# Sixteen decode buffers in the memory of a ring that starts later, both gates from tanh, and signs made off VectorE, in a top-32 attention and two gated feed-forward layers

## The chip, the cores and the metric

The kernel runs on one core of a Trainium2 chip. Its engines are TensorE (PE, matmuls; its weight loads are shown as PEld), VectorE (DVE), ScalarE (ACT), GpSimd (POOL), and SyncE (SP), whose queue issues the DMAs. Each engine works through its own instructions in the order in which they stand in the program, and waits on semaphores of the others. The metric is the device time of one execution in microseconds. Before the change three runs took 1339.08, 1341.06 and 1344.63 us, so the median is 1341.06 us.

## The reference

Inputs are q, k, v of 4 batches x 8 heads x 576 rows x 64, and two sets of weights, w_gate and w_val (512 x 1536) and w_out (1536 x 512). q, k, v and the output are float32, the weights float64.

```
scores = 0.125 * q @ k.T
keep the 32 largest scores of each row, the rest becomes -1e9
attn = exp(scores - max); attn = attn / (sum(attn) + 1e-9)
x = attn @ v, laid out as 2304 tokens x 512
x = (silu(x @ w_gate) * (x @ w_val)) @ w_out           # first layer
out = (sigmoid(x @ w_gate2) * (x @ w_val2)) @ w_out2   # second layer
```

silu(g) is g times sigmoid(g).

## The kernel before, in words

The 2304 tokens are 36 tiles of 64 tokens and are worked on in six chunks of 4, 5, 6, 7, 7 and 7 tiles (SIZES). For each chunk there is an attention part and then the two feed-forward layers, called MoE below. A head pair is handled at a time, so that 64 tokens of two heads make a row tile of 128 rows; each chunk has four row tiles for each of its tiles, 144 in all.

The attention of a row tile runs over all engines. PE makes the scores (ps_s, line 575), ACT copies them to s (lines 581, 588). DVE finds the 32nd largest of each row with four MAX8 and three MATCH_REPLACE8 passes (lines 729, 731), ACT makes e = exp(s - max) (line 687), and DVE masks and sums it in one pass, p = (s >= 32nd) * e with the row sum as a second output (line 695). A small add, a reciprocal (lines 699, 703) and a scaling by it follow. PE transposes p (ps_t, line 762) and multiplies by v (ps_v, line 781).

Chunk 0 and the other chunks handle weights in different ways. The kernel reads the weights from DRAM as they are, 8 bytes each, and makes float32 of them itself. In chunk 0 (mode N) `decode` loads each half of a slab into `wr` (512 KB, a ring of 3), decodes it into `wf` (a ring of WF = 8) with passes on ACT (line 453), a sign and a low part in `wu` by DVE, ACT or POOL (lines 457, 468, 472, 478, 480), and a merge on DVE (line 483). There are 36 slabs of two halves, 72 in all. Every decoded half is stored to DRAM as `sw` (line 487), and chunk 0's matmuls read `wf` itself as plain float32 (`ps_m<-xn,wf` and `ps_m<-hn,wf`, line 805). In the later chunks (mode P) the halves are loaded back as `raw` and split on the chip in a high and a low part, w[:, 0] and w[:, 1] (lines 434, 436, 439), and each product is three matmuls (high by high, low by high, high by low; `xh`, `xl`, `hh`, `hl`).

Memory has two phases. Rings of phase 0 (`xn`, `hn`, `wr`, `wf`, `wu` and others) belong to chunk 0, rings of phase 1 (`xh`, `xl`, `hh`, `hl`, `raw`) take the same place once every buffer of phase 0 is done. The ring `w` of the split weights, 4 buffers of 8 KB per partition, lay outside both.

Scores of three head pairs of chunk 5 are made ahead of time (EARLY = "000003", buffers `ke`, `qe`, `se`) and parked in DRAM (`ss`, line 561).

The order of all work is not written out by hand. A planner (class Plan) takes operations with a duration, a priority and a sequence number, plays them through on a model of the engines, and emits them in the order in which it started them. A ring hands out its buffers in the order in which the program asked for them. So constants such as P_DEC, and the durations given to `op`, decide what stands next to what; nothing is reordered while the kernel runs.

In the MoE, `moe` takes f = 0 to 11: a group of matmuls for the gate (4 in chunk 0, 12 later) goes to one of three PSUM buffers `ps_m`, ACT turns it into `sil` by Silu in the first layer and Sigmoid in the second (line 834), a second group makes the value, and DVE multiplies the two (lines 843, 851). Silu, Sigmoid and Exp sit in different tables of ACT, and a change of table is an ACT_TABLE_LOAD.

## Time and profile before

| | |
|---|---|
| median of three runs | 1341.06 us |
| the profiled execution's own time | 1339.5 us |
| its span, first to last instruction | 1337.7 us |
| PE busy | 1252.6 us, 94% |
| PEld busy | 1030.6 us, 77% |
| DVE busy | 1105.1 us, 83% |
| ACT busy | 911.2 us, 68% |
| POOL busy | 775.2 us, 58% |
| DMA | 194.19 MB, mean 145 GB/s |
| mean granted TensorE clock | 0.981 |

Busy is the time in which at least one instruction of the engine was under way. Matmuls overlap in their pipeline, so PE's busy time alone does not say how near it is to its peak: where PE is busy all the time, what counts is the pace from one matmul to the next. The shares are averages over stages that differ much: chunk 0's attention up to 116 us, chunk 0's MoE with chunk 1's attention up to 333 us, then the other chunks, and from 1040 us on MoE alone.

### The profile page before, as it was taken

What the parts mean: (1) busy time and instruction counts of PE and PEld (TensorE: products, weight loads), DVE (VectorE), ACT (ScalarE), POOL (GpSimd) and SP (SyncE); (2) the same over time, 40 slices, a digit from 0 to 9 for tenths busy, and PEclk for the clock granted to TensorE, in tenths of its full rate; (3) what the DMA queues carried; (4) which work ended last, traced back from release to release, by engine and by line L of the source; (5) the groups of instructions that cost most, each with busy time, mean ns of one, the idle gap of its engine ahead of it and who ended that gap; (6) DMA issues with size and microseconds to landing.
All of it is one profiled execution on the core that took longest, in us unless ns stands there. A gap on an engine that the chain in (4) does not pass through costs nothing.

```text
span 1337.7 us, 22187 instructions
## 1 busy us (share of the span) xinstructions
PE 1252.6 (94%) x7504; PEld 1030.6 (77%) x7504; DVE 1105.1 (83%) x2325; ACT 911.2 (68%) x1592; POOL 775.2 (58%) x841
## 2 busy tenths in 40 slices
PE   4478988887999999999999999999999999999998
PEld 1235666555888888888888887899888899999998
DVE  7994999998999999999999999999999455344442
ACT  6566878796997988986896877688678333332331
POOL 4101444433997987875887676699677445343431
PEclk9868999998999999999999999999999999999999
DMA  8245888886343444433334333444522223433231
GB/s 271 91 141 184 258 253 265 268 269 229 130 136 129 143 130 135 136 107 122 113 106 154 103 101 125 147 137 134 182 79 78 97 98 107 147 102 123 98 111 67
DMA packets 93426, 194.19 MB, mean 145 GB/s; under 512 B 10369, under 2 KB 17537, under 8 KB 93313
## 3 DMA queue, kind: packets, MB, share of 16 engines
q1 hardware_dynamic: 93312, 192.78, 44.1%
q8 instruction: 59, 0.97, 0.3%
q14 instruction: 55, 0.44, 0.1%
HBM read 162.96 MB, written 29.79 MB: 144 GB/s over the span
## 4 chain that ended last, share of the span: by engine, by line
PE 74%; ACT 7%; DMA 6%; DVE 4%; issue 1%; POOL 1%; SPq 0%; ACTq 0%; POOLq 0%; DVEq 0%
PE ps_m L805 59%; PE ps_v L781 5%; PE ps_s L575 5%; PE ps_t L762 5%; DMA wr<-in_wall_dram 3%; DVE st L729 1%; ACT L834 1%; DMA sw<-wf 1%; DVE wk L731 1%; DMA raw<-sw 1%; ACT wf L453 1%; ACT L687 1%; DVE p L695 1%; ACT e L687 1%; DMA ss<-se 1%
## 5 line engine op out<-in xcount | busy, mean ns | idle before, releaser
L439 POOL TENSOR_TENSOR w<-raw,w 128x512 fp32r<-128x512 f32 x297 | 404.9, 1372 | 23.2 <-ACT w L434 16.9
L805 PE MATMUL ps_m<-xh,w 128*128 128x448 f32 (+2 forms) x1920 | 403.2, 351 | 1.5 <-ACT sil L834 1.3
L805 PEld LDWEIGHTS ps_m<-xh,w 128*128 128x128 f32 x1920 | 334.9, 188 | 38.2 <-issue 13.9
L729 DVE MAX8 st<-wk 128x8 f32<-128x576 f32 x432 | 312.4, 745 | 0.1
L436 POOL TENSOR_SCALAR w<-raw 128x512 fp32r<-128x512 f32 x169 | 111.9, 666 | 246.8 <-PE ps_m L805 128.2
L434 ACT ACTIVATE w<-raw 128x512 fp32r<-128x512 f32 x191 | 119.7, 628 | 148.4 <-PE ps_m L805 117.3
L805 PE MATMUL ps_m<-xl,w 128*128 128x448 f32 (+2 forms) x960 | 216.0, 346 | 0.4 <-POOL xl L439 0.4
L731 DVE MATCH_REPLACE8 wk<-st,wk 128x576 f32<-128x576 f32 x288 | 212.4, 739 | 0.0
L805 PE MATMUL ps_m<-hh,w 128*128 128x448 f32 (+2 forms) x960 | 201.2, 351 | 0.0
L805 PEld LDWEIGHTS ps_m<-hh,w 128*128 128x128 f32 x960 | 167.7, 188 | 16.5 <-issue 7.6
L805 PEld LDWEIGHTS ps_m<-xl,w 128*128 128x128 f32 x960 | 172.1, 188 | 8.1 <-POOL xl L439 0.7
L695 DVE SCALAR_TENSOR_TENSOR p<-s,st,e 128x576 f32<-128x576 f32 x144 | 157.6, 1094 | 0.1
L575 PE MATMUL ps_s<-k,q 64*64 64x288 f32 x984 | 104.8, 462 | 34.4 <-ACT s L581 29.7
L439 DVE TENSOR_TENSOR w<-raw,w 128x512 fp32r<-128x512 f32 x63 | 70.3, 1118 | 79.8 <-POOL w L436 61.0
L762 PE MATMUL ps_t<-ident,p 128*128 128x128 f32 (+1 forms) x736 | 115.6, 287 | 14.6 <-ACT p L708 11.0
L762 PEld LDWEIGHTS ps_t<-ident,p 128*128 128x128 f32 (+1 forms) x736 | 87.8, 144 | 53.4 <-ACT p L708 18.7
L851 DVE TENSOR_TENSOR h<-sil,ps_m 128x448 f32<-128x448 f32 (+2 forms) x120 | 69.0, 575 | 72.1 <-PE ps_m L805 63.4
L768 ACT ACTIVATE pt<-ps_t 128x512 f32<-128x512 f32 (+3 forms) x256 | 105.6, 438 | 18.5 <-PE ps_t L762 17.4
L687 ACT ACTIVATE e<-s,st 128x576 f32<-128x576 f32 x144 | 111.6, 775 | 3.8 <-POOL st L683 1.8
L729 DVE MAX8 st<-s 128x8 f32<-128x576 f32 x144 | 106.7, 742 | 8.0 <-ACT s L581 8.0
L805 PE MATMUL ps_m<-hl,w 128*128 128x448 f32 (+2 forms) x480 | 107.9, 346 | 0.0
L731 DVE MATCH_REPLACE8 wk<-st,s 128x576 f32<-128x576 f32 x144 | 106.3, 739 | 0.0
(57 smaller groups left out, 1636.5 us busy)
## 6 DMA issues: line engine op xcount, KB each, us to landing
raw<-sw SPq DMA_DIRECT2D x360, 256.0 KB, 2.8
wr<-in_wall_dram SPq DMA_DIRECT2D x72, 512.0 KB, 4.8
sw<-wf SPq DMA_DIRECT2D x72, 256.0 KB, 5.2
...
```

The costliest lines, as they stand in the source:

```text
L434: nc.scalar.activation(out=hi(), in_=raw(), func=AF.Copy)
L436: nc.gpsimd.tensor_scalar(hi(), raw(), 1.0, 1.0, op0=ALU.mult, op1=ALU.mult)
L439: (nc.gpsimd if eng == "pool" else nc.vector).tensor_sub(lo(), (lo_raw or raw)(), lo_hi() if lo_hi else f32(hi()))
L575: nc.tensor.matmul(psg[y:y + 64, h, :288], qg[r, (o + j) * 64:(o + j + 1) * 64], kg[r, x * 288:x * 288 + 288], start=True, stop=True)
L687: nc.scalar.activation(out=eg[:], in_=src(), func=AF.Exp, bias=stg[:, 32:33], scale=SCALE)
L695: nc.vector.scalar_tensor_tensor(out=o, in0=src(), scalar=stg[:, 31:32], in1=eg[:], op0=ALU.is_ge, op1=ALU.mult, accum_out=stg[:, 33:34])
L729: nc.vector.max(out=stg[:, 4 * k:4 * k + 8], in_=src() if k == 0 else wk())
L731: nc.vector.match_replace(out=wk(), in_to_replace=stg[:, 4 * k - 4:4 * k + 4], in_values=src() if k == 1 else wk(), imm_value=NEG)
L762: nc.tensor.transpose(tg[:width, i], pg[:, a:a + width], ident)
L768: nc.scalar.activation(out=dst(), in_=src(), func=AF.Copy)
L805: nc.tensor.matmul(pg[:, :n], blk(a, d), src(x, d), start=first and i == 0, stop=last and i == 4 * len(terms) - 1)
L851: nc.vector.tensor_mul(h32[:, :n], sg[:, :n], pg[:, :n])
```

## The change

Five things are changed together.

- `wf` has 16 buffers in place of 8 and `wr` 4 in place of 3. The ring `w` moves into phase 1.
- All 72 signs are made by ACT and POOL (SP = 4 in place of 2), none by DVE.
- Both gates use Tanh with scale 0.5, which lies in the table of Exp: sigmoid(g) = (1 + tanh(g/2)) / 2. In the first layer a new pass on DVE makes (t + 1) * g in place, and the value's product stays a plain multiplication; in the second layer the product on DVE becomes (t + 1) * value. The factor 1/2 is taken in the copies of the outputs.
- In chunk 0 the row tile masks before the exponential: DVE writes -3e38 where a score is under the 32nd (`cut`), POOL adds the scores, and ACT makes the exponential and the row sum in one pass.
- The early scores are called for two at a time after each row-tile pair of chunk 0's attention, from the third on, and no longer at the start of chunk 0's MoE. Some durations that the planner is told are changed.

```
-E_FIRST = 64
+E_FIRST = 0
+E_SKIP = 2
+E_LAST = 1
+E_IN = [2, 1, 0, 0, 0, 0]
+BEFORE = [1, 0, 0, 0, 0, 0]
+WR = 4
-E_DMA = 7
-SP = 2
+E_DMA = 5
+SP = 4
-WF = 8
+WF = 16
...
-        "w": ring("w", [P, 2, 8, P], F32R, W),
...
+            specs["w"] = ([P, 2, 8, P], F32R, W)
...
-            b = op("pool", 588, s2, deps=[b], uses=[g], allocs=[u], prio=prio)
+            b = op("pool", 775, s2, deps=[b], uses=[g], allocs=[u], prio=prio)
...
-            a = op("pe", 50 + 287 * 2, qk, deps=lds, uses=[kg, qg], allocs=[psg], prio=pq)
+            a = op("pe", 840, qk, deps=lds, uses=[kg, qg], allocs=[psg], prio=pq)
...
+                tiles[0] += 1
+                if tiles[0] > E_SKIP:
+                    step(E_IN[c])
...
+        def cut():
+            take(eg)
+            nc.vector.tensor_scalar(eg[:], src(), stg[:, 31:32], NEG, op0=ALU.is_lt, op1=ALU.mult)
+
+        def add():
+            nc.gpsimd.tensor_tensor(out=eg[:], in0=eg[:], in1=src(), op=ALU.add)
+
+        def ex_sum():
+            take(pg)
+            nc.scalar.activation(out=pg[:, e * S:(e + 1) * S], in_=eg[:], func=AF.Exp, bias=stg[:, 32:33],
+                                 scale=SCALE, accum_out=stg[:, 33:34])
...
+    def gated(out, t, x):
+
+
+        nc.vector.scalar_tensor_tensor(out=out, in0=t, scalar=1.0, in1=x, op0=ALU.add, op1=ALU.mult)
+
+    def product(out, gate, val, moe_i):
+        if moe_i == 0:
+            nc.vector.tensor_mul(out, gate, val)
+        else:
+            gated(out, gate, val)
...
-                                nc.scalar.activation(out=sg[:, :n], in_=pg[:, :n],
-                                                     func=AF.Silu if moe_i == 0 else AF.Sigmoid)
+                                nc.scalar.activation(out=sg[:, :n], in_=pg[:, :n], func=AF.Tanh, scale=0.5)
+                            g_op = op("act", act_ps(n), ev, deps=[m], uses=[pg], allocs=[sg], prio=0, table="exp")
+                            if moe_i == 0:
+                                def silu(pg=pg, sg=sg, n=n):
+                                    gated(sg[:, :n], sg[:, :n], pg[:, :n])
+                                g_op = op("dve", dve(n), silu, deps=[g_op], uses=[pg, sg], prio=0)
...
-                            nc.scalar.activation(out=nx[0][:, m_i, o:o + n], in_=pg[:, :n], func=AF.Copy)
+                            nc.scalar.activation(out=nx[0][:, m_i, o:o + n], in_=pg[:, :n], func=AF.Copy, scale=0.5)
...
-        step(1000)
-
+        if c >= E_LAST:
+            step(1000)
```

The first place is SP's queue around the start of chunk 0's MoE. `wr_n` is the n-th half slab on its way in, `sw` its decoded form on its way out, `v_5` the second V of chunk 1, `ss` parked early scores. Before:

```order
L561 DMA ss3_2_4_163<-se_9_983 128x1152
L427 DMA v_5_1013<-in_vL_dram 128x640
L427 DMA wr_11_1036<-in_wall_dram 128x1024
L487 DMA sw4_66<-wf_8_1027 128x512
L427 DMA wr_12_1051<-in_wall_dram 128x1024
```

And now:

```order
L493 DMA sw7_69<-wf_15_653 128x512
L567 DMA ss3_2_6_161<-se_10_966 128x1152
L567 DMA ss3_2_8_162<-se_11_997 128x576
L433 DMA v_4_1087<-in_vL_dram 128x640
L433 DMA k_6_1123<-in_kT_dram 128x576
L433 DMA q_6_1134<-in_qT_dram 128x320
L433 DMA v_5_1253<-in_vL_dram 128x640
L433 DMA wr_20_1303<-in_wall_dram 128x1024
L493 DMA sw8_70<-wf_16_1292 128x512
```

Eleven loads of weights (wr_0 to wr_10) stood ahead of `v_5`, and twenty (wr_0 to wr_19) do now; eight stores stood there, and sixteen do now. 61 loads and 64 stores were left, and 52 and 56 are now.

The second place is DVE's queue at the end of chunk 0's attention: st_15 and row tile 15 are the last of chunk 0, `s_8` and later belong to chunk 1. Before:

```order
L695 SCALAR_TENSOR_TENSOR p_7_931,st_15_912<-s_7_621,st_15_912,e_15_924 128x576
L699 TENSOR_SCALAR st_15_912<-st_15_912 128x1
L703 RECIPROCAL st_15_912<-st_15_912 128x1
L483 SCALAR_TENSOR_TENSOR wf_8_1027<-wf_8_1027,wu_2_296 128x512
L843 TENSOR_TENSOR hn_0_1045<-sil_0_1034,ps_m_1_1029 128x256
L483 SCALAR_TENSOR_TENSOR wf_9_1048<-wf_9_1048,wu_0_266 128x512
```

And now, without the 19 rows of chunk 1's row tiles between the two pieces:

```order
L699 TENSOR_SCALAR e_15_1167<-s_7_927,st_15_1105 128x576
L758 MAX st_16_1143<-wk_16_1150 128x8
L758 MAX st_17_1174<-s_8_1026 128x8
L760 MATCH_REPLACE wk_16_1150<-st_16_1143,wk_16_1150 128x576
L760 MATCH_REPLACE wk_17_1180<-st_17_1174,s_8_1026 128x576
L758 MAX st_16_1143<-wk_16_1150 128x8
L731 RECIPROCAL st_15_1105<-st_15_1105 128x1
...
L723 SCALAR_TENSOR_TENSOR p_9_1283,st_18_1209<-s_9_1073,st_18_1209,e_18_1220 128x576
L822 SCALAR_TENSOR_TENSOR sil_0_1290<-sil_0_1290,ps_m_0_1273 128x256
```

The merge of half slab 8, which stood next behind the last row tile, now stands long ahead of it, and passes of chunk 1's row tiles fill the place. PE's own queue has the same 215 rows up to the first matmul of chunk 1's MoE (`ps_m<-xh`), with the same counts of each kind; of these, 140 score matmuls and 72 transposes stood ahead of chunk 0's first MoE matmul, and 184 and 80 do now.

The third place is DVE's queue at the first two gates of chunk 1's MoE. `sil` is the gate, `h32` its product with the value. Before:

```order
L729 MAX st_39_2957<-wk_39_2987 128x8
L851 TENSOR_TENSOR h32_4_3012<-sil_24_2972,ps_m_57_2974 128x320
L729 MAX st_38_2903<-wk_38_2914 128x8
L731 MATCH_REPLACE wk_39_2987<-st_39_2957,wk_39_2987 128x576
L695 SCALAR_TENSOR_TENSOR p_21_3033,st_38_2903<-s_21_2600,st_38_2903,e_38_2927 128x576
```

And now:

```order
L822 SCALAR_TENSOR_TENSOR sil_24_3070<-sil_24_3070,ps_m_56_3036 128x320
L758 MAX st_38_3002<-wk_38_3012 128x8
L826 TENSOR_TENSOR h32_4_3091<-sil_24_3070,ps_m_57_3052 128x320
L760 MATCH_REPLACE wk_38_3012<-st_38_3002,wk_38_3012 128x576
L760 MATCH_REPLACE wk_39_3119<-st_39_3073,s_21_2697 128x576
```

A pass on DVE has come between ACT's gate and the product, and it reads the same PSUM buffer as the gate did. ACT's queue has one ACT_TABLE_LOAD where it had 137.

## Rows read from the trace of the kernel before

**Rows 1.** Windows by stage: us, busy (instructions) of each engine, PEclk, DMA share, GB/s
```profile
0.00:116.20 116.20, 67.50 (x432) 28.36 (x432) 98.59 (x221) 68.41 (x127) 20.51 (x44) 0.82 0.48 164
116.20:333.20 217.00, 188.10 (x1024) 133.57 (x1021) 192.05 (x409) 171.86 (x304) 89.71 (x122) 0.98 0.81 254
333.20:1040.00 706.80, 703.08 (x4578) 595.97 (x4577) 685.89 (x1542) 573.76 (x996) 552.12 (x567) 1.00 0.38 125
1040.00:1337.70 297.70, 293.89 (x1478) 272.73 (x1477) 128.59 (x155) 97.22 (x166) 112.83 (x109) 1.00 0.31 106
```
**Rows 2.** Timeline of PE at both seams: start us, us, engine line op
```profile
116.22 1.99 PE L805 MATMUL ps_m<-xn,wf 128*128 128x256 f32 x8
118.15 0.71 PE L575 MATMUL ps_s<-ke,qe 64*64 64x288 f32 x8
...
333.22 1.42 PE L805 MATMUL ps_m<-xh,w 128*128 128x320 f32 x8
```
**Rows 3.** Waits of PE, 116 to 333 us: total us, times, longest
```profile
PE ps_m L805 <- DVE wf L483: 12.6, 9, 4.2
...
PE ps_m L805 <- ACT sil L834: 4.3, 3, 2.5
```
**Rows 4.** Groups by line of PE from 333.3 us: busy, mean ns | idle before
```profile
L805 PE MATMUL ps_m<-xh,w 128*128 128x448 f32 (+2 forms) x1920 | 403.2, 351 | 1.5 <-ACT sil L834 1.3
```
**Rows 5.** Groups by line of DVE, 0 to 116.2 us
```profile
L695 DVE SCALAR_TENSOR_TENSOR p<-s,st,e 128x576 f32<-128x576 f32 x16 | 12.9, 803 | 0.1
...
L483 DVE SCALAR_TENSOR_TENSOR wf<-wf,wu 128x512 int32<-128x512 int32 x8 | 6.5, 818 | 0.0
...
L457 DVE TENSOR_SCALAR wu<-wf 128x512 int32<-128x512 int32 x4 | 2.0, 507 | 0.1
```
**Rows 6.** Groups by line of DVE, 116.2 to 333.2 us
```profile
L483 DVE SCALAR_TENSOR_TENSOR wf<-wf,wu 128x512 int32<-128x512 int32 x64 | 46.7, 736 | 21.1 <-ACT wf L453 13.9 <-POOL wu L480 5.0 <-ACT wu L478 1.3
...
L695 DVE SCALAR_TENSOR_TENSOR p<-s,st,e 128x576 f32<-128x576 f32 x21 | 18.6, 884 | 0.0
...
L457 DVE TENSOR_SCALAR wu<-wf 128x512 int32<-128x512 int32 x32 | 14.6, 456 | 7.1 <-ACT wf L453 7.0
L843 DVE TENSOR_TENSOR hn<-sil,ps_m 128x256 f32<-128x256 f32 x24 | 10.0, 416 | 5.6 <-PE ps_m L805 3.9 <-ACT sil L834 1.4
```
**Rows 7.** Timeline of DVE: last masks of chunk 0 and chunk 1
```profile
105.81 0.82 DVE L695 SCALAR_TENSOR_TENSOR p<-s,st,e 128x576 f32<-128x576 f32 x1
...
118.96 0.69 DVE L483 SCALAR_TENSOR_TENSOR wf<-wf,wu 128x512 int32<-128x512 int32 x1 [11.94 <-ACT wf L453]
...
322.12 0.80 DVE L695 SCALAR_TENSOR_TENSOR p<-s,st,e 128x576 f32<-128x576 f32 x1
```
**Rows 8.** Groups by line, whole kernel
```profile
L439 POOL TENSOR_TENSOR w<-raw,w 128x512 fp32r<-128x512 f32 x297 | 404.9, 1372 | 23.2 <-ACT w L434 16.9
...
L695 DVE SCALAR_TENSOR_TENSOR p<-s,st,e 128x576 f32<-128x576 f32 x144 | 157.6, 1094 | 0.1
...
L687 ACT ACTIVATE e<-s,st 128x576 f32<-128x576 f32 x144 | 111.6, 775 | 3.8 <-POOL st L683 1.8
...
L834 ACT ACT_TABLE_LOAD x70 | 89.8, 1283 | 1.1
...
L687 ACT ACT_TABLE_LOAD x66 | 84.7, 1283 | 1.2
...
L851 DVE TENSOR_TENSOR h<-sil,ps_m 128x448 f32<-128x448 f32 (+2 forms) x120 | 69.0, 575 | 72.1 <-PE ps_m L805 63.4 <-issue 2.7 <-ACT sil L834 1.9
...
L472 POOL TENSOR_SCALAR wu<-wg 128x512 int8<-128x512 int8 x36 | 29.5, 823 | 49.2 <-ACT wg L468 43.7 <-DVE wk L731 3.2 <-ACT st L681 2.0
```
**Rows 9.** Timeline of SP's queue behind `v_5`
```profile
118.95 0.33 SPq L427 DMA_DIRECT2D wr<-in_wall_dram  x1
```
**Rows 10.** Instructions on tiles wr and wf: ns min/median/max, first and last start us
```profile
L427 SPq DMA_DIRECT2D wr<-in_wall_dram x72: 327/328/632, 3.5 to 304.0; - x72
...
L483 DVE SCALAR_TENSOR_TENSOR wf<-wf,wu x72: 665/688/1186, 15.6 to 317.4; 128x512 int32<-128x512 int32 x72
```

More of the change, by code (lines that the diff above doesn't have):

```diff
@@ L657, in segment @@
                     done = score_ops(sg, [sg], kg, qg, lds, o, m, P_QK, P_S)
-                norms = [row_tile(sg, new("st"), done, e, pg) for e in range(m)]
+                norms = [row_tile(sg, new("st"), done, e, pg, BEFORE[c]) for e in range(m)]
+                tiles[0] += 1
+                if tiles[0] > E_SKIP:
+                    step(E_IN[c])
                 for k3 in range(3):
@@ L670, in score_load, with row_tile @@
         return op("dma", dma(P * S * 4 * m), fn, deps=[st], allocs=[sg], prio=2, lat=DMA_LAT)
-    def row_tile(sg, stg, a, e, pg):
+    def row_tile(sg, stg, a, e, pg, before):
         eg = new("e")
@@ L683, in neg @@
                 nc.gpsimd.tensor_scalar(stg[:, 32:33], stg[:, 0:1], -SCALE, 1.0, op0=ALU.mult, op1=ALU.mult)
+        m0 = op({"act": (180, P_EX), "pool": (200, P_EX)}, 0, neg, deps=[m0], uses=[stg])
+        def cut():
[7 more added lines that the diff above has]
+                                 scale=SCALE, accum_out=stg[:, 33:34])
         def ex():
@@ L688, in ex @@
                                  bias=stg[:, 32:33], scale=SCALE)
-        m0 = op({"act": (180, P_EX), "pool": (200, P_EX)}, 0, neg, deps=[m0], uses=[stg])
-        x = op("act", act(S), ex, deps=[m0], uses=[sg, stg], allocs=[eg], prio=P_EX, table="exp")
+        if before:
+            x = op("dve", 380, cut, deps=[last], uses=[sg, stg], allocs=[eg], prio=P_MASK, lock=True)
+            x = op("pool", pool_tt(S), add, deps=[x], uses=[sg, eg], prio=P_CUT)
+            y = op("act", act(S), ex_sum, deps=[m0, x], uses=[eg, stg], allocs=[pg], prio=P_EX, table="exp")
+        else:
+            x = op("act", act(S), ex, deps=[m0], uses=[sg, stg], allocs=[eg], prio=P_EX, table="exp")
         def mask():
@@ L710, in norm @@
                 nc.gpsimd.tensor_scalar(o, o, stg[:, 35:36], 1.0, op0=ALU.mult, op1=ALU.mult)
-        y = op("dve", 729, mask, deps=[last, x], uses=[sg, stg, eg], allocs=[pg], prio=P_MASK, lock=True)
+        if not before:
+            y = op("dve", 729, mask, deps=[last, x], uses=[sg, stg, eg], allocs=[pg], prio=P_MASK, lock=True)
         y = op({"dve": (69, P_MASK), "pool": (200, P_MASK)}, 0, eps, deps=[y], uses=[stg])
@@ L762, in tr @@
                 nc.tensor.transpose(tg[:width, i], pg[:, a:a + width], ident)
-        t = op("pe", 57 + pe(len(o), 128), tr, deps=deps, uses=[pg], allocs=[tg], prio=P_PT)
+        t = op("pe", 5 + pe(len(o), 128), tr, deps=deps, uses=[pg], allocs=[tg], prio=P_PT)
         out = []
@@ L782, in go @@
                                      ptg[:, 8 if i == 4 else 4 * h + i, :W], start=(i == 0), stop=(i == 4))
-        a = op("pe", 95 + 10 * max(W / 1.2 + 3, 110), go, deps=pt_ops + [v_ld], uses=[ptg, vg], allocs=[og], prio=P_PV)
+        a = op("pe", 200 + 10 * max(W / 1.2 + 3, 110), go, deps=pt_ops + [v_ld], uses=[ptg, vg], allocs=[og], prio=P_PV)
         def cp():
@@ L807, in mms @@
                     i += 1
-        if c == 0:
+        if c == 0 and E_FIRST:
             step(E_FIRST)
@@ L847, in moe, with mul @@
                         h32 = new("h32")
-                        def mul(pg=pg, sg=sg, h32=h32, n=n):
+                        def mul(pg=pg, sg=sg, h32=h32, n=n, moe_i=moe_i):
                             take(h32)
-                            nc.vector.tensor_mul(h32[:, :n], sg[:, :n], pg[:, :n])
+                            product(h32[:, :n], sg[:, :n], pg[:, :n], moe_i)
                         v = op("dve", dve(n), mul, deps=[m, s_op], uses=[pg, sg], allocs=[h32], prio=0)
@@ L898, in cp @@
                             take(ob)
-                            nc.scalar.activation(out=ob[:, :n], in_=pg[:, :n], func=AF.Copy)
+                            nc.scalar.activation(out=ob[:, :n], in_=pg[:, :n], func=AF.Copy, scale=0.5)
                         def st(ob=ob, m_i=m_i, o=o, n=n):
```

25 lines of the change are left out of this document (15 added, 10 removed).

## The prediction

> **What bounds the kernel now.** I read the windows by stage first, then the seams in PE's timeline, then what ended the waits on each side of the seams. In the windows [rows 1] the reader is to see three stages. Up to 116.2 us PE is busy for 67.5 us and DVE for 98.6: chunk 0's attention, carried by DVE. From 116.2 to 333.2 us PE is busy for 188.1 of 217.0 us, DVE for 192.1, ACT for 171.9, and DMA runs at 0.81 of its time and 254 GB/s: four resources near their limit together, none at it. From 333.2 us on PE is busy for 997.0 of 1004.5 us at a granted clock of 1.00. The seams are the first matmul of chunk 0's MoE at 116.22 and of chunk 1's at 333.22 us [rows 2]. So the time is A + M + L = 116.2 + 217.0 + 1004.5 = 1337.7 us of span, and the execution's own 1339.5 us have 1.8 us around that. The sum below is made against 1339.5, which lies 1.6 us under the median and inside the three runs; I leave that difference alone.
>
> **L, the 1004.5 us behind the second seam.** PE's queue has the same rows on either side of this seam in both kernels, so L moves only by waits that go or come. The costliest group of PE's matmuls there stood idle for 1.5 us in all, of which 1.3 for the gate [rows 4]. The change takes 136 table loads of 1.283 us [rows 8] from ACT, 174 us, most of them in this stage, but ACT is busy 573.8 of 706.8 us there and PE hardly waits for it. That is worth 0 to 3 us, and I take 0. It adds 60 gate passes on DVE in the five later chunks (12 each), at the 0.575 us of the product that also reads PSUM [rows 8]: 34.5 us. DVE is busy 685.9 of 706.8 us before 1040 us, but only 128.6 of 297.7 behind it [rows 1]. It finishes the attention long before PE needs the last of it, and 34.5 us fit there. What it costs if a gate comes late is a rival below.
>
> **A, up to the first matmul of chunk 0's MoE.** DVE sets it. Sixteen masks of 0.803 us with their sum's read-out of about 0.08 go: -14.1. Sixteen cuts come; no row shows one. It has one large input, as the integer pass for the sign has, 0.507 us for 512 elements [rows 5], or 0.57 for 576: +9.1. The dearest it should be is the mask that it replaces, 0.803 (+12.8), and the cheapest the like pass of the second stage, 0.456 unscaled [rows 6] (+7.3); I take the middle row because it is the same engine's one-input pass in the same stage. Four signs go, -2.0, and eight more merges of 0.818 [rows 5] stand ahead of the last row tile, +6.5. The sum is -0.5 us, so the last pass starts at 105.3 where the mask stood at 105.81 [rows 7]. From the mask to the first matmul it was 10.4 us. That chain now has an add on POOL, by the 1.372 us for 512 elements [rows 8] 1.54, and behind it the exponential of 0.775 [rows 8], which before ran beside the rounds; against that the last DVE pass is 0.23 shorter. So +2.1, and the seam lies at 117.8. The 20 loads and 16 stores ahead of it are 9 x 0.512 and 8 x 0.256 MB more than before, some 26 MB in all with the 164 GB/s that this stage moved [rows 1]; 224 GB/s are asked for where the next stage got 254, so a little lateness is likely. I take 119, and 114 (the chain hidden) to 126 (ACT held by late loads in its own order) as bounds.
>
> **M, between the seams.** Three floors, each from its own rows.
>
> PE: 188.1 us busy, less what now stands ahead of the first seam: 44 score matmuls at 0.71 for 8 [rows 2], 3.9 us, and 8 transposes, about 1.2. That leaves 183.0. It was idle for 28.9 us, of which 12.6 for a merged weight and 4.3 for a gate [rows 3]. With 16 decoded halves at the start, each of which feeds 8 matmuls in 1.99 us [rows 2], I take these two away and half of the other 12.0: 183 + 6 = 189.
>
> The weight stream: loads went out from 118.95 [rows 9] to 304.0 us [rows 10], 61 of them, so one in 3.08 us. From the last load to the last merge at 317.4 it was 13.4 us [rows 10], from there to the second seam 15.8. At the old pace the 52 that are left take 51 x 3.08 = 157, and 2.7 + 157 + 13.4 + 15.8 = 189.
>
> DVE: from the last mask of chunk 0 at 105.81 to that of chunk 1 at 322.12 [rows 7] 216.3 us. The hole of 11.9 us in front of 118.96, where the merge of half slab 8 stood first in DVE's queue and waited for a buffer of `wf`, is filled by chunk 1's rounds. 32 signs of 0.456 go, -14.6, the eight moved merges of 0.736 go, -5.9, and 12 gate passes of 0.416 come, +5.0 [rows 6]. That is 188.9 from 105.3, so 294.2, and 11.1 us on (333.2 - 322.1) the seam: 305, before the other floors' 308.
>
> So the second seam lies at 119 + 189 + 1 for three floors that lie so near each other: 309 us, where it was 333.2. POOL gets 25 more of the 36 added signs in this stage at 0.823 us [rows 8], 20.6 us beside 89.7 busy of 217, and ACT as many at about the same price against some 20 table loads fewer; neither becomes the bound.
>
> The ring `w` in phase 1 costs nothing: `raw`, from which it is filled, lay in phase 1 already, so no split could start sooner. If that cover were gone, it would be one load, split and product in a row at the second seam, some 3 us.
>
> The sum: 1339.5 + (309 - 333.2) = 1315.3, and with A and M at their bounds (114 + 183, and 126 + 195) 1303 to 1327. I forecast 1315 us.
>
> A row shows a mask pass, which has two inputs in on-chip memory, at 0.803 us where POOL is busy 20.5 of 116.2 us, at 0.884 where it is busy 89.7 of 217.0, and at 1.094 over the whole kernel, where POOL is busier still [rows 1, 5, 6, 8]. The Trainium skill (GPSIMD Engine Reference, section Specifications) says that GpSimd shares its SBUF interfaces with VectorE, and that they get in each other's way when VectorE runs with two SBUF inputs or in a mode that uses both ports. The masks agree; the merges, 0.818 and then 0.736, do not. This speaks against moving signs and adds to POOL, and it is the second rival.
>
> **The rivals.**
>
> 1. *Everything overlaps.* DVE's hole and its stalls on weights go, the stream runs faster with four `wr`, and PE's 183 us are all that is left behind a seam at 116: 299, so 1305, and 1300 if the longer chain and the late loads cost nothing either and the cut half of what I take (first seam 111). For it: DMA stood at 0.81, not at 1. Against it: four resources at 79 to 88% seldom line up.
>
> 2. *POOL slows DVE.* 52 merges and 20 masks of M, and 16 merges of A, each stretched by the 0.21 us between 0.884 and 1.094: 88 x 0.21 = 18.5 us. DVE's 305 becomes 323, the time 1329. For it the masks' rows, against it the merges'.
>
> 3. *The early loads hold up chunk 0's attention.* ACT decodes in a fixed order, and a late load holds the score copies behind it, so DVE starves. If the 9 added loads cost 2 us each, the first seam is at 137 and the second, with the same 189, at 326: 1332. The point from which it decides is a wait of ACT for `wr` of over 15 us before the first seam.
>
> 4. *The gates hold PE up in L (slower).* The gate's PSUM buffer is now let go by DVE's pass and not by ACT. There are three, and a group of 12 matmuls takes some 2.1 us (1.5 x 1.42 [rows 2]), so PE needs it back about 4 us behind the end of its own group. ACT's gate, a wait in DVE's queue for one or two 0.74 us passes and the 0.575 are mostly under that. If that room is gone and each of the 60 passes shows once, PE loses 34.5 us: 1350. If each also stood behind a whole mask of 1.094, 100 us: 1415. For it: DVE 97% busy. Against it: a table load of 1.283 us often stood ahead of the same gate and made no wait.
>
> 5. *The change does not do what it says:* chunk 1's attention sets the seam whatever the weights do, and DVE's other idle time grows by as much as was saved. Then 1336 to 1342.
>
> **How the numbers follow.** The forecast (1306 to 1326) 0.58, rival 1 0.14, rivals 2 and 3 together 0.14, rival 5 0.08, rival 4 0.06. About 0.5%, 6.7 us, is what a measurement of this kernel can tell from no change. Faster by more than that means under 1334.4: the forecast, rival 1 and most of rivals 2 and 3, 0.85. Within it: rival 5 and a little of 3, 0.09. Slower: rival 4, 0.06. The range of 8 in 10 leaves out the better half of rival 1 and the slow end: 1299 to 1336. The forecast's own is 1306 to 1326.
>
> **What will show it.** The second seam (first `ps_m<-xh`) near 309 us and the first (`ps_m<-xn`) near 119; L at 1004 us again, with PE's waits there under 5 us; no idle stretch of DVE at the end of chunk 0's attention; PE's wait for merged weights in M near nothing; masks in M under 0.95 us. I am wrong if the first seam is past 130, if the pace of loads falls well over 3.1 us, or if L grows by more than 10 us.

## The result and the profile after

The changed kernel took 1319.77 us (median of four runs, 1319.1 to 1323.15), the kernel before beside it 1340.32 us. The ratio is 0.9846 with a 95% interval from 0.9818 to 0.9874. I had predicted 1315 us, 1299 to 1336. The profiled execution took 1319.67 us, its span is 1317.9 us.

The windows by stage of the kernel after, cut at its own seams; the columns are those of [rows 1].

```profile
0.00:133.30 133.30, 86.92 (x529) 34.30 (x530) 117.17 (x251) 94.57 (x188) 62.08 (x84) 0.80 0.60 207
133.30:306.00 172.70, 167.64 (x926) 128.73 (x924) 164.32 (x345) 138.52 (x271) 98.57 (x132) 1.00 0.81 270
306.00:1014.00 708.00, 705.49 (x4571) 595.45 (x4570) 695.61 (x1551) 453.35 (x931) 525.17 (x522) 1.00 0.38 125
1014.00:1317.90 303.90, 300.39 (x1486) 273.83 (x1484) 142.68 (x192) 97.00 (x171) 117.11 (x115) 1.00 0.31 103
```

With the names of the prediction, A went from 116.2 to 133.3 us (+17.1), M from 217.0 to 172.7 (-44.3), and L from 1004.5 to 1011.9 (+7.4). The sum is -19.8, the difference of the two spans. The second seam lies at 306.0, where 309 was forecast, but the first at 133.3, where 119 was.

The seams in PE's timeline, which answer to [rows 2]:

```profile
133.26 1.89 PE L845 MATMUL ps_m<-xn,wf 128*128 128x256 f32 x8
...
305.61 0.66 PE L791 MATMUL ps_t<-ident,p 128*128 128x128 f32 x4 [2.52 <-ACT p L736]
306.04 1.41 PE L845 MATMUL ps_m<-xh,w 128*128 128x320 f32 x8
```

What PE waited for between the seams, 133.3 to 306 us, the whole answer (total us, times, longest):

```profile
PE ps_t L791 <- ACT p L736: 2.8, 2, 2.5
PE ps_s L581 <- ACT s L587: 2.1, 3, 1.0
PE ps_s L581 <- ACT s L594: 0.2, 1, 0.2
```

The waits for merged weights (12.6 us) and for gates (4.3 us) of [rows 3] are gone. The wait that stands last before the second seam is a transpose's for `p`. In the program's order this `p` is that of row tile 36, the first of chunk 2, whose transposes stand ahead of chunk 1's first MoE matmul in PE's queue, as they did before the change. So the wait does not tell by itself what sets the seam, and I cut the stage M once more, where the last group of chunk 0's MoE starts (294.8 us, the last matmul with `wf` in it):

```profile
133.30:294.80 161.50, 160.07 (x863) 124.80 (x862) 153.12 (x318) 130.62 (x252) 92.78 (x124) 1.00 0.82 272
294.80:306.00 11.20, 7.57 (x65) 3.93 (x63) 11.20 (x28) 7.90 (x19) 5.79 (x8) 1.00 0.70 240
```

In the last 11.2 us DVE (the third pair) is busy from end to end and PE is not. Most of that DVE work is chunk 2's already. DVE takes the row tiles in their order, so the last mask of chunk 1, that of row tile 35, is the 36th cut or mask in its queue:

```profile
295.12 0.80 DVE L723 SCALAR_TENSOR_TENSOR p<-s,st,e 128x576 f32<-128x576 f32 x1
```

The last group of chunk 0's MoE (294.8) and the last mask of chunk 1 (295.1) come together, and the seam is 10.9 us behind the mask. Between them lie the scaling of `p`, the transposes, the product with V and the split of `x`; in this tail ACT also stands 2.4 us for a load of `raw`, ahead of its copy of `x`. Before, the mask stood at 322.12 [rows 7], the seam 11.1 us behind it, and the last group of chunk 0's MoE (ns min/median/max, first and last start) at 321.2:

```profile
L805 PE MATMUL ps_m<-hn,wf x192: 379/379/796, 178.0 to 321.2; 128*128 128x256 f32 x192
```

So weights and rounds ended almost together before the change; they do so again, both 26 to 27 us earlier.

The groups of DVE that answer to [rows 5] (first fence, 0 to 133.3 us) and [rows 6] (second, 133.3 to 306 us):

```profile
L489 DVE SCALAR_TENSOR_TENSOR wf<-wf,wu 128x512 int32<-128x512 int32 x16 | 13.5, 858 | 2.4 <-POOL wu L486 2.1
L699 DVE TENSOR_SCALAR e<-s,st 128x576 f32<-128x576 f32 x16 | 9.6, 607 | 0.0
```

```profile
L489 DVE SCALAR_TENSOR_TENSOR wf<-wf,wu 128x512 int32<-128x512 int32 x56 | 43.3, 784 | 2.8 <-ACT wf L459 1.7 <-POOL wu L486 0.5 <-issue 0.2
L723 DVE SCALAR_TENSOR_TENSOR p<-s,st,e 128x576 f32<-128x576 f32 x19 | 17.3, 910 | 0.0
L822 DVE SCALAR_TENSOR_TENSOR sil<-sil,ps_m 128x256 f32<-128x256 f32 x12 | 4.9, 411 | 3.4 <-ACT sil L874 3.4
```

A cut costs 0.607 us (0.57 was taken), a gate pass 0.411 (0.416), a merge 0.858 and 0.784 where it was 0.818 and 0.736. Waits before merges fell from 21.1 to 2.8 us in M. Up to the second seam DVE was busy for 98.59 + 192.05 = 290.6 of 333.2 us before and for 281.5 of 306.0 after: 9.1 us less work and 18.1 us less idle time.

The costliest groups of PE's matmuls from 306 us on, which answer to [rows 4], and below them DVE's gate passes of the same stretch:

```profile
L845 PE MATMUL ps_m<-xh,w 128*128 128x448 f32 (+2 forms) x1920 | 407.3, 354 | 0.1
L845 PE MATMUL ps_m<-xl,w 128*128 128x448 f32 (+2 forms) x960 | 217.9, 348 | 0.0
```

```profile
L822 DVE SCALAR_TENSOR_TENSOR sil<-sil,ps_m 128x448 f32<-128x448 f32 (+2 forms) x60 | 34.2, 569 | 7.2 <-ACT sil L874 6.9
```

The same 1920 matmuls took 351 ns each before and take 354 now, at a granted clock of 1.00 both times. PE waits for no gate (idle 0.1 us), so L did not grow by rival 4.

### The profile page after: what moved, and what is told of

It is laid out like the page before. It is cut to its first block, busy times and chain, and to the rows that moved or that the text cites. A ratio compares the mean times of both kernels' runs of the same rounds, so it can differ in the third digit from the quotient of the medians.

```text
span 1317.9 us, 22208 instructions
## 1 busy us (share of the span) xinstructions
PE 1260.4 (96%) x7504; PEld 1032.3 (78%) x7504; DVE 1119.8 (85%) x2335; ACT 783.4 (59%) x1559; POOL 802.9 (61%) x852
## 4 chain that ended last, share of the span: by engine, by line
PE 70%; DVE 14%; ACT 6%; DMA 5%; POOL 3%; issue 3%; SPq 0%; POOLq 0%; DVEq 0%; ACTq 0%
PE ps_m L845 55%; PE ps_s L581 5%; DVE st L758 5%; PE ps_t L791 5%; PE ps_v L810 4%; DVE wk L760 4%; DMA wr<-in_wall_dram 3%; DVE p L723 2%; POOL w L445 1%; ACT wf L459 1%; DMA raw<-sw 1%; ACT wg L474 1%; ACT s L587 1%; POOL wu L478 1%; DVE wf L489 1%
## 5 line engine op out<-in xcount | busy, mean ns | idle before, releaser
L445 POOL TENSOR_TENSOR w<-raw,w 128x512 fp32r<-128x512 f32 x301 | 411.0, 1374 | 36.5 <-ACT w L440 26.1
L845 PE MATMUL ps_m<-xh,w 128*128 128x448 f32 (+2 forms) x1920 | 407.3, 354 | 0.1
L440 ACT ACTIVATE w<-raw 128x512 fp32r<-128x512 f32 x225 | 140.9, 629 | 189.1 <-PE ps_m L845 146.8
L442 POOL TENSOR_SCALAR w<-raw 128x512 fp32r<-128x512 f32 x135 | 86.5, 642 | 250.5 <-PE ps_m L845 136.3
L723 DVE SCALAR_TENSOR_TENSOR p<-s,st,e 128x576 f32<-128x576 f32 x128 | 144.6, 1129 | 0.0
L445 DVE TENSOR_TENSOR w<-raw,w 128x512 fp32r<-128x512 f32 x59 | 65.9, 1118 | 74.6 <-POOL w L442 55.6
L791 PE MATMUL ps_t<-ident,p 128*128 128x128 f32 (+1 forms) x736 | 117.4, 290 | 11.2 <-ACT p L736 8.9
L874 ACT ACTIVATE sil<-ps_m 128x448 f32<-128x448 f32 (+3 forms) x144 | 70.1, 487 | 87.3 <-PE ps_m L845 86.6
L711 ACT ACTIVATE e<-s,st 128x576 f32<-128x576 f32 x128 | 98.8, 773 | 3.2 <-POOL st L694 1.3
```

What stands on the lines that cost most here:

```text
L440: nc.scalar.activation(out=hi(), in_=raw(), func=AF.Copy)
L442: nc.gpsimd.tensor_scalar(hi(), raw(), 1.0, 1.0, op0=ALU.mult, op1=ALU.mult)
L445: (nc.gpsimd if eng == "pool" else nc.vector).tensor_sub(lo(), (lo_raw or raw)(), lo_hi() if lo_hi else f32(hi()))
L711: nc.scalar.activation(out=eg[:], in_=src(), func=AF.Exp, bias=stg[:, 32:33], scale=SCALE)
L723: nc.vector.scalar_tensor_tensor(out=o, in0=src(), scalar=stg[:, 31:32], in1=eg[:], op0=ALU.is_ge, op1=ALU.mult, accum_out=stg[:, 33:34])
L791: nc.tensor.transpose(tg[:width, i], pg[:, a:a + width], ident)
```

## The experiments

Each run undoes or isolates one part of the change. Each ratio is to the kernel before, run beside it on the same chip. Seams, busy times and medians of all runs stand in the table at the end of this section.

**The changed kernel again**, as a base for the others.

> The changed kernel again, as it is, beside the runs of the same chip. Both theories: 1319 to 1323 us. Its profile asks whether the last stage's slower pace comes with the kernel or with the execution: chunk 5's first MoE layer took 86 us before the change and 87.5 and 89.4 us for the two layers after. If the pace belongs to the kernel, this profile shows 1008 to 1012 us behind the second seam again; if it belongs to the execution, it can come back to 1004.

1320.72 us, ratio 0.983 (0.9807 to 0.9853); seams 132.4 and 307.5. The seams repeat within 1.5 us. L is 1011.0 us again, so its slower pace belongs to the kernel and not to one execution.

**Decode buffers back to 8 and 3**, `w` still in phase 1.

```
-WF = 16
+WF = 8
-WR = 4
+WR = 3
```

> The changed kernel with 8 wf and 3 wr buffers again. Theory of the passes (the second seam is where DVE has worked off its passes up to the last mask of chunk 1, near gapless): no pass comes or goes, the order has chunk 1's rounds ready at the first seam, so 1319 to 1324 us. Rival (the buffers are what matters): DVE waits for buffers of wf at the first seam again, 12 us, and PE for merged weights as before the change, so 1332 to 1340 us.

1336.82 us, ratio 0.9947 (0.9924 to 0.9969). The rival was right. The first seam comes back to 116.6, the second goes to 324.5. PE waits for weights again:

```profile
PE ps_m L845 <- DVE wf L489: 12.5, 12, 1.7
```

The passes over `wr` and `wf`, first of this kernel, then of the changed one (ns min/median/max, first and last start):

```profile
L433 SPq DMA_DIRECT2D wr<-in_wall_dram x72: 327/328/432, 6.7 to 304.6; - x72
L489 DVE SCALAR_TENSOR_TENSOR wf<-wf,wu x72: 667/690/1892, 16.4 to 313.5; 128x512 int32<-128x512 int32 x72
```

```profile
L433 SPq DMA_DIRECT2D wr<-in_wall_dram x72: 327/328/622, 6.0 to 279.0; - x72
L489 DVE SCALAR_TENSOR_TENSOR wf<-wf,wu x72: 660/692/1886, 16.4 to 285.4; 128x512 int32<-128x512 int32 x72
```

With 8 buffers the last load goes out at 304.6, as before [rows 10], with 16 at 279.0. Chunk 1's last mask stands at 289.7 here, 26 us ahead of chunk 0's last group (316.2), so the weights alone set this seam. The weight stream is one of two things that can set it, and 16 `wf` with 4 `wr` buffers bring its end forward by some 26 us. The two rings were not tried apart.

**The same, with `w` outside the phases again**, as the kernel before had it.

```
+        "w": ring("w", [P, 2, 8, P], F32R, W),
...
-            specs["w"] = ([P, 2, 8, P], F32R, W)
```

> As the run with 8 and 3 buffers, but with the ring w outside the phases again, where it lay before the change. It asks for the last stage's pace: 448-column matmuls came every 200 us/1000 before, every 203 to 205 ns in every kernel with w in phase 1. Theory (place in memory): pace 200 to 201 ns again, last stage 6 to 10 us shorter, 1327 to 1331 us against 1337. Rival (the pace comes with other parts of the change, such as the gate passes): 203 to 205 ns, 1334 to 1339 us.

1329.78 us, ratio 0.9886 (0.9861 to 0.9911), against 0.9947 with `w` in phase 1; the intervals do not touch. L is 1003.3 us against 1008.8. The costliest PE group from the second seam on, first with `w` in phase 1, then outside:

```profile
L845 PE MATMUL ps_m<-xh,w 128*128 128x448 f32 (+2 forms) x1920 | 408.2, 354 | 0.1
```

```profile
L845 PE MATMUL ps_m<-xh,w 128*128 128x448 f32 (+2 forms) x1920 | 403.8, 352 | 0.4 <-DVE sil L822 0.3
```

Where `w` lies changes PE's pace in L. By the medians that is some 7 us of the time; the two profiled executions differ by 2.1 us alone, for L is 5.5 us shorter here and the second seam 3.4 us later. So the buffers with the move of `w`, which makes room for them, are worth only 5 us (by the ratios) to 10 us (1329.78 against 1319.77), while the buffers by themselves are worth the 14 to 17 of the run above.

**16 buffers, `w` as the first ring of phase 1**, so that `xh`, `xl`, `hh` and `hl` lie where the kernel before had them.

```
+        if kinds & {"S", "P", "R"}:
+            specs["w"] = ([P, 2, 8, P], F32R, W)
         if kinds - {"N"}:
```

> The changed kernel with w as the first ring of phase 1 and not the last: xh, xl, hh, hl and raw then lie at the addresses that they had before the change, w 64 KB below its new place. If the place of the x and h rings sets the pace: 200 to 201 ns and 1310 to 1314 us. If w's place does, or neither: 203 ns and more, 1318 to 1323 us.

1324.45 us, ratio 0.9856 (0.9836 to 0.9876), no better than the changed kernel. The group above stands at 354 ns again. So it is not the place of the moving operand that costs the pace. What about the place of `w` does, stays open: with `w` gone from the permanent rings, those behind it (`sil`, `h32`, `s` and the others) also lie 32 KB lower in each of these kernels, and the two were not told apart.

**36 signs on DVE again.**

```
-SP = 4
+SP = 2
```

> The changed kernel with half of the signs on DVE again (36 passes of 0.46 us, 16.4 us on DVE before the second seam; 36 passes fewer on POOL and ACT). Theory of the passes: the second seam moves from 306 to about 322 and the time to 1334 to 1338 us. Rival (buffers and the weight stream decide, DVE has room): 1317 to 1323 us.

1329.98 us, ratio 0.9895 (0.9873 to 0.9916): +9 to +10 us, between the two forecasts, though 36 signs of 0.456 us [rows 6] are 16.4 us. DVE was busy for 293.5 us up to the second seam in place of 281.5, 12.0 more; the 72 merges took 52.5 us in place of 56.8, with POOL busy for 129.2 us in place of 160.7. The seam went to 315.9. Chunk 0's last group started at 290.7, but chunk 1's last mask only at 300.8, so here DVE's passes decide. The window from the last group to the seam shows DVE busy in all of it, PE in 14 us:

```profile
290.70:315.90 25.20, 14.04 (x86) 6.35 (x84) 25.20 (x60) 16.61 (x35) 17.45 (x17) 0.72 0.58 187
```

Only 5.7 of the 9.9 us lie ahead of the mask. Behind it the tail is 15.1 us in place of 10.9: one more group of chunk 2's scores stands ahead of the first `xh` matmul in PE's queue and waits 2.7 us for ACT.

**Silu and Sigmoid again, no gate passes** and no factors 1/2, the planner told of the tables as before.

```
...
-nc.scalar.activation(out=sg[:, :n], in_=pg[:, :n], func=AF.Tanh, scale=0.5)
+nc.scalar.activation(out=sg[:, :n], in_=pg[:, :n], func=AF.Silu if moe_i == 0 else AF.Sigmoid)
...
-                     ... prio=0, table="exp")
+                     ... prio=0, table="silu" if moe_i == 0 else "sigmoid")
```

> The changed kernel with Silu and Sigmoid again, without the gate passes on DVE and without the factors 1/2. Theory of the passes: 12 passes of 0.41 us, 5 us, leave DVE before the second seam, ACT gets some 20 table loads, 26 us, beside 233 us busy of 306; DVE sets the seam, so 1314 to 1323 us. Rival (the table loads held the kernel up): 1328 to 1340 us.

1349.87 us, ratio 1.0034 (1.0014 to 1.0053): +29 us, and slower than the kernel before. My theory, by which the gates cost next to nothing, fell. Between the seams PE waits for gates as for nothing else:

```profile
PE ps_m L842 <- ACT sil L871: 18.2, 7, 6.0
```

The profile is that of this kernel's longest run, 1355.35 us, so its seams fit the median to some 5 us only.

**Tanh on the chip, but the planner told of Silu's and Sigmoid's tables**, so that the instructions are those of the changed kernel, with one table load, and only their order is another.

```
-                     ... prio=0, table="exp")
+                     ... prio=0, table="silu" if moe_i == 0 else "sigmoid")
```

> The changed kernel, still with Tanh for both gates and one table load, but the planner is told that the gates need tables of their own, as before, so it defers gates behind work of the current table. Undoing the gates as a whole cost 29 us, against what the theory of the passes said. New theory (order): the gates' cost is not the 1.283 us loads but that the planner holds a gate back in ACT's order for as long as exponentials and their like are there; gates then start 2 us and more behind their matmuls again and the time is 1332 to 1345 us. Rival (loads): without loads on the chip the order costs little, 1319 to 1326 us.

1348.96 us, ratio 1.004 (1.0025 to 1.0055). The same +29 us without the 126 loads: the order by itself costs that much. What the loads of the run above add, and what its missing gate passes on DVE give back, the two runs do not tell apart. The planner holds an operation back that needs another table as long as operations of the present one are at hand, up to HOLD = 8000 ns, so exponentials go ahead of gates. The window between the seams of this kernel:

```profile
132.50:336.60 204.10, 185.48 (x1018) 136.38 (x1016) 194.53 (x415) 152.98 (x298) 104.55 (x146) 0.97 0.72 233
```

The last groups of chunk 0's MoE (first and last start at the end of the numbers), here and then in the changed kernel:

```profile
L845 PE MATMUL ps_m<-hn,wf x192: 379/379/547, 203.3 to 328.9; 128*128 128x256 f32 x192
```

```profile
L845 PE MATMUL ps_m<-hn,wf x192: 379/379/483, 186.0 to 294.8; 128*128 128x256 f32 x192
```

Chunk 0's MoE ends 34 us later. PE's hole shows only in part as a wait: 92 more rows of later attention fill it (1018 against 926), and DVE does 415 passes there against 345. I also counted from the traces how long ACT's 24 gates of chunk 0 began behind the end of their own matmuls: 51.5 us in all before, 13.1 after, 67.4 here, and 93.9 in the run above, where loads stand ahead of them as well.

**Silu and Sigmoid on the chip, the planner told of one table**, so that no gate is held back. Gate passes and factors are left out here too.

```
-nc.scalar.activation(out=sg[:, :n], in_=pg[:, :n], func=AF.Tanh, scale=0.5)
+nc.scalar.activation(out=sg[:, :n], in_=pg[:, :n], func=AF.Silu if moe_i == 0 else AF.Sigmoid)
```

> Silu and Sigmoid on the chip as in the run with the old gates, so with their table loads, but the planner is not told of tables and places the gates at once. Theory (order): the loads alone cost little, 1322 to 1334 us although there are more of them. Rival (loads): as with the old gates or worse, 1345 us and more.

1378.5 us, ratio 1.0254 (1.0236 to 1.0273): +58 us. The theory of the order (1322 to 1334) fell here, and the rival, by which the loads cost (1345 and more), was right. ACT's timeline shows a pair of the 152 loads on both sides of one exponential:

```profile
341.44 0.21 ACT L692 ACTIVATE st<-st 128x1 f32<-128x1 f32 x1
341.68 1.28 ACT L711 ACT_TABLE_LOAD   x1
342.97 0.78 ACT L711 ACTIVATE e<-s,st 128x576 f32<-128x576 f32 x1
343.65 0.45 ACT L440 ACTIVATE hh<-h 128x320 fp32r<-128x320 f32 x1
344.12 1.28 ACT L871 ACT_TABLE_LOAD   x1
345.42 0.44 ACT L871 ACTIVATE sil<-ps_m 128x320 f32<-128x320 f32 x1
```

L grew to 1047.6 us here, with ACT busy for 704.5 us of it in place of 550.3 and PE waiting for its copies (14.4 us for scores, 10.6 for transposes), so the loads stand in the way in L too as soon as the order does not reckon with them. With two tables one pays either for holding back or for loads. The rows put a switch at 1.28 us: the load starts 0.03 us behind the end of the instruction before it, and the next starts 0.01 us behind the load. The Trainium skill (ScalarE: Activation LUTs, What ACT_TABLE_LOAD costs) adds a drain of about 1.38 us to each switch, 2.66 in all; no row here shows one.

**Early scores back at the start of chunk 0's MoE.**

```
-E_FIRST = 0
+E_FIRST = 64
-E_IN = [2, 1, 0, 0, 0, 0]
+E_IN = [0, 0, 0, 0, 0, 0]
```

> Only the early scores go back to where the kernel before had them, at the start of chunk 0's MoE. DVE's passes are the same in number, so if DVE's sum sets the second seam it stays at 305 to 308 us, the first seam comes earlier (ACT has 36 score copies less before it), about 122 to 128 us, and the time is 1318 to 1324 us. The rival, that the early scores were what made the first seam late and that this lateness is paid in full: first seam near 119, time 1308 to 1312 us. A second rival, that PE's busy time between the seams (167.6 of 172.7 us) leaves no room for 36 more score matmuls: 1325 to 1335 us.

1341.37 us, ratio 0.9979 (0.9963 to 0.9995): some 20 us slower than the changed kernel, more than any theory gave. The windows of this kernel, cut at its seams and at the last group of chunk 0's MoE:

```profile
0.00:126.00 126.00, 70.08 (x424) 29.55 (x424) 101.10 (x213) 83.73 (x166) 58.37 (x76) 0.84 0.60 201
126.00:294.50 168.50, 163.19 (x885) 123.34 (x882) 143.63 (x301) 133.13 (x254) 89.64 (x117) 1.00 0.83 272
294.50:331.70 37.20, 23.60 (x148) 11.51 (x148) 37.20 (x84) 22.86 (x49) 18.07 (x22) 0.68 0.40 133
```

Chunk 0's MoE ends at 294.5, as in the changed kernel. DVE's work up to the second seam is the same, 101.10 + 143.63 + 37.20 = 281.9 us against 281.5, and its idle time is 49.8 us against 24.5. These 25.3 us more idle are the 25.7 us by which the seam is late. What DVE waited for between the seams:

```profile
DVE sil L822 <- ACT sil L874: 15.6, 4, 10.1
DVE wf L489 <- ACT wf L459: 7.6, 10, 1.6
```

DVE's timeline shows the longest of these waits and the first pass on chunk 1:

```profile
128.48 0.42 DVE L822 SCALAR_TENSOR_TENSOR sil<-sil,ps_m 128x256 f32<-128x256 f32 x1 [10.09 <-ACT sil L874]
...
143.20 1.42 DVE L758 MAX8 st<-s 128x8 f32<-128x576 f32 x2 [0.41 <-ACT s L587]
```

PE and ACT make and copy early scores around the first seam, ACT's copies of scores from 101 to 138 us are all of these, chunk 1's own scores stand behind them, and DVE has nothing but gates and merges to wait for. In the changed kernel DVE had masked two row tiles of chunk 1 before its first seam. Chunk 1's last mask comes at 321.3 here, 27 us behind the last group of chunk 0's MoE.

**Masks after the exponential in chunk 0 again.**

```
-BEFORE = [1, 0, 0, 0, 0, 0]
+BEFORE = [0, 0, 0, 0, 0, 0]
```

> Chunk 0's row tiles mask after the exponential again, as the kernel before did: 16 masks of about 0.88 us for 16 cuts of 0.607 us on DVE, and POOL loses 16 adds of 1.49 us. If the sum of DVE's passes sets the second seam, as it seems from DVE's 24 us of idle time in 306 us, the seam moves by +4 to +5 us and the time is 1323 to 1326 us. The rival, that POOL's adds cost as much as they save (a longer chain at the first seam, slower passes on DVE): the first seam comes 2 us earlier and the time is 1314 to 1320 us.

1319.0 us, ratio 0.9797 (0.9764 to 0.9829). The rival was right on the time (1314 to 1320 us): the cut is worth nothing, and costs a little if anything (the interval touches those of the changed kernel). DVE has 287.6 us of work up to the second seam, 6.1 more, and the first seam comes 8.5 us sooner, not 2. Chunk 1's last mask stands at 295.0, as in the changed kernel; the seam is 14.5 us behind it, at 309.5, with a group of scores in the way as with the signs (1.9 us), and L is 2 to 3 us shorter.

**The cut in chunk 1 too**, for a better version.

```
-BEFORE = [1, 0, 0, 0, 0, 0]
+BEFORE = [1, 1, 0, 0, 0, 0]
```

> Chunk 1's 20 row tiles cut before the exponential too, with the add on POOL. DVE saves 20 times about 0.3 us ahead of the second seam, 6 us; POOL gets 20 adds of 1.49 us, 30 us beside 98.6 busy of 172.7. If DVE's sum alone sets the seam: 300 to 302 us and 1313 to 1316 us in all. If PE is as near a floor as it looks (167.6 busy of 172.7 us) or the longer chain through POOL takes the gain back: 1317 to 1322 us. If POOL, which also makes signs, becomes late: over 1324 us.

1319.31 us, ratio 0.9813 (0.9783 to 0.9844): no gain. The merges between the seams (131.5 to 308.6 us) show where most of it went:

```profile
L489 DVE SCALAR_TENSOR_TENSOR wf<-wf,wu 128x512 int32<-128x512 int32 x56 | 47.9, 874 | 1.9 <-ACT wf L459 1.1 <-ACT wu L484 0.4 <-POOL wu L478 0.3
```

18 cuts of 0.586 us in place of masks of 0.910 save 5.8 us there. The 56 merges cost 47.9 - 43.3 = 4.6 us more, with POOL busy for 119.2 of 177.1 us in place of 98.6 of 172.7. The Trainium skill (GPSIMD Engine Reference, Specifications) says that GpSimd gets in VectorE's way when VectorE reads two SBUF inputs. A merge does, and between these two kernels it agrees, 0.784 to 0.874 us. What is left shows in chunk 1's last cut, 1.6 us sooner at 293.5; the seam is 15.0 us behind it, for POOL's add now stands in the chain, and a group of chunk 2's scores in PE's queue again (1.9 us).

**The kernel before with the tanh gates alone.**

```
-func=AF.Silu if moe_i == 0 else AF.Sigmoid)
+func=AF.Tanh, scale=0.5)
...
-table="silu" if moe_i == 0 else "sigmoid"))
+table="exp")
```

> The kernel before with the tanh gates alone: one table, the gate passes on DVE, everything else as before (8 decode buffers, 36 signs on DVE, masks after the exponential). If one table saves what its undoing cost, whatever the buffers: 29 us, 1312 to 1318 us. If the floors lie so close together that a part alone gains little, because 8 buffers and 5 us more on DVE hold the second seam: 1328 to 1341 us. If the gate passes cost more than the order gives back: over 1345 us.

1339.81 us, ratio 0.9966 (0.995 to 0.9982): 3 to 5 us of the 29. ACT's gates are on time (8.4 us in all for chunk 0's 24, where it was 51.5), but with 8 buffers the last merge is at 325.1 and the seam at 333.1:

```profile
L483 DVE SCALAR_TENSOR_TENSOR wf<-wf,wu x72: 665/684/1203, 15.6 to 325.1; 128x512 int32<-128x512 int32 x72
```

All runs side by side. "MoE" is the start of the last matmuls with `wf`, "mask" that of chunk 1's last mask or cut (row tile 35); the second seam is 4 to 15 us behind the later of the two. DVE's idle time is the second seam less its busy time up to there; L is the span less the second seam.

| kernel | first seam | MoE | mask | second seam | DVE busy, idle | L | median |
|---|---|---|---|---|---|---|---|
| before (8 buffers) | 116.2 | 321.2 | 322.1 | 333.2 | 290.6, 42.6 | 1004.5 | 1340.3 |
| 8 buffers | 116.6 | 316.2 | 289.7 | 324.5 | 295.2, 29.3 | 1008.8 | 1336.8 |
| 8 buffers, `w` outside | 118.7 | 319.5 | 293.0 | 327.9 | 293.8, 34.1 | 1003.3 | 1329.8 |
| before with tanh (8 buffers) | 118.9 | 328.6 | 322.7 | 333.1 | 292.0, 41.1 | 1003.7 | 1339.8 |
| after (16 buffers) | 133.3 | 294.8 | 295.1 | 306.0 | 281.5, 24.5 | 1011.9 | 1319.8 |
| after again | 132.4 | 296.2 | 296.4 | 307.5 | 280.9, 26.6 | 1011.0 | 1320.7 |
| `w` first in phase 1 | 131.6 | 296.5 | 296.6 | 306.8 | 278.9, 27.9 | 1015.9 | 1324.5 |
| masks as before | 124.8 | 286.0 | 295.0 | 309.5 | 287.6, 21.9 | 1008.8 | 1319.0 |
| cut in chunk 1 too | 131.5 | 295.3 | 293.5 | 308.6 | 287.0, 21.6 | 1008.0 | 1319.3 |
| signs as before | 129.3 | 290.7 | 300.8 | 315.9 | 293.5, 22.4 | 1012.3 | 1330.0 |
| early scores as before | 126.0 | 294.5 | 321.3 | 331.7 | 281.9, 49.8 | 1009.1 | 1341.4 |
| gates as before | 133.8 | 343.8 | 294.6 | 348.7 | 310.8, 37.9 | 1004.7 | 1349.9 |
| only the order of those gates | 132.5 | 328.9 | 294.5 | 336.6 | 311.6, 25.0 | 1011.2 | 1349.0 |
| only their tables | 133.1 | 317.0 | 314.0 | 328.4 | 280.5, 47.9 | 1047.6 | 1378.5 |

## Why the prediction was right in sum, and where not

**The second seam, 309 forecast, 306.0 measured: the mechanism right, the number in part by luck.** 309 was summed as A + M = 119 + 189 + 1. A came out 14.3 us longer and M 17.3 us shorter, and the two nearly cancel. What held is DVE's floor, the one that was put in time from the start: chunk 1's last mask forecast at 294.2 and measured at 295.1, the seam 11.1 us behind it by forecast and 10.9 measured. Its terms were off too. Up to that mask DVE had 279.6 us of work and 42.6 idle before; the forecast's terms make 263.5 and 30.7, and 270.6 and 24.5 came. Of the 7.1 us of work that did not go, 3.6 are the dearer merges (56.8 us in place of 53.2).

That chunk 1's passes on DVE decide when the weights do not is shown by the signs (mask at 300.8, chunk 0's last group at 290.7) and by the early scores (321.3 and 294.5; no work more, 25.3 us more idle, seam +25.7). That the weights or the gates decide when they are late is shown by the 8 buffers (mask at 289.7, last group at 316.2) and by the order of the gates (294.5 and 328.9). In the changed kernel both end together.

**The weight stream: the mechanism right, its size off.** It was put beside DVE's sum at 3.08 us for a load. From the first load behind the seam at 136.2 to the last at 279.0 it ran at 142.8 / 51 = 2.8. All four kernels with 8 buffers have chunk 0's last group at 316 to 329 us, those with 16 buffers and the tanh gates in their new order at 286 to 297.

**A, 119 forecast, 133.3 measured: mis-sized by 14 us.** The last cut stood at 119.42 where 105.3 was forecast, in a row with chunk 1's passes:

```profile
118.77 0.74 DVE L760 MATCH_REPLACE8 wk<-st,wk 128x576 f32<-128x576 f32 x1
119.42 0.51 DVE L699 TENSOR_SCALAR e<-s,st 128x576 f32<-128x576 f32 x1
119.85 0.75 DVE L758 MAX8 st<-wk 128x8 f32<-128x576 f32 x1
```

Up to there DVE waited 3.5 us for POOL's small adds, 2.1 for POOL's low parts and 2.1 for an exponential, and passes of chunk 1 stand ahead of the cut. In all it was busy for 103.3 us and idle for 16.1 up to the last cut, where it had been 97.5 and 8.4 up to the last mask: 5.8 and 7.8 us more, where -0.5 was forecast for both together. The step that failed is therefore the sum of DVE's passes in A. The chain behind the last pass took 13.8 us, where 12.5 and 1.2 for late loads were taken; in it ACT stood 3.9 us for a buffer of chunk 1's scores, ahead of its last copy to `xn`. By the prediction's own sign (wrong if the first seam is past 130) this part was wrong. The hole of 11.9 us, though, is gone: from the last cut to the first seam DVE is busy for 13.9 of 13.9 us.

PE's part was mis-sized as well. I had put 44 more score matmuls at 3.9 us; the trace has two records for each, and scores took 55.9 us ahead of the seam where it had been 39.5. PE did 19.4 us of work more ahead of the first seam, where 5.1 was taken, and so its floor in M is 167.6 us in place of 183:

```profile
L581 PE MATMUL ps_s<-k,q 64*64 64x288 f32 x200 | 28.4, 639 | 25.1 <-ACT s L587 15.0 <-DMA q<-in_qT_dram 4.1 <-ACT se L587 2.1
L581 PE MATMUL ps_s<-ke,qe 64*64 64x288 f32 x168 | 27.5, 657 | 14.8 <-ACT se L587 8.8 <-ACT s L587 4.1 <-ACT se L594 1.8
```

The miss was not paid in the end: M was 17 us shorter than forecast, since work of DVE and PE that was taken for M stood ahead of the first seam. With 8 buffers, with masks or with early scores as before the first seam came 7 to 17 us sooner, and two of these three kernels were slower all the same.

**L unchanged: wrong by 7.4 us.** "The ring `w` in phase 1 costs nothing" is the step that failed. PE was busy for 8.9 us more (705.49 + 300.39 against 703.08 + 293.89 [rows 1]) with the same matmuls, and putting `w` back outside gives 5.5 us of L. The prediction asked only when the splits could start, not how fast the matmuls would read them.

**Gates valued at next to nothing: wrong by 29 us.** The step that takes 0 for the table loads looked at L, where PE waited 1.3 us for gates in all [rows 4], and at the loads' own time; in M it took away 4.3 us of gate waits and counted some 20 loads fewer on ACT. The gates' worth is in M, and it is the order that one table allows. It is also worth that much only where 16 buffers have made room: alone it gave 3 to 5 us.

**Early scores: not priced at all,** beyond the rows that they move ahead of the first seam. Undone, they cost some 20 us.

So the total came near (A +14.3, M -17.3, L +7.4 us against the forecast's terms) because DVE's chain to chunk 1's last mask ended where it was forecast, and because the misses on either side of the first seam cancelled. That the weights were out of the way by then rests on gates and early scores that the forecast had valued at next to nothing. Undone one by one the parts cost 16 (buffers), 9 (signs), 29 (gates) and 20 us (early scores), 74 in all, where all together gained 20.6. These are not shares of the gain. The stream, DVE's chain and the gates' order each hold the second seam at 316 to 349 us as soon as one of them is back, and only with all out of the way does it come to 306.

Rival 1 (everything overlaps) fell: the first seam was at 133.3, not 116, and DVE's chain was left. Rival 2 (POOL slows DVE) is true in kind: merges dearer by 0.04 to 0.05 us in both stages, some 3.6 us in 72 (56.8 against 53.2), where it had put 0.21 us each. Rival 3 (late loads) did not show: ACT waited 2.5 us for `wr` ahead of the first seam, where it decides from 15. Rivals 4 and 5 fell: no gate wait of PE in L, and a seam 27 us sooner.
